# Attention and a routed expert layer on one core: w1 loaded in halves, five matmuls ahead of the first transposes, q's halves loaded ahead of k's, and v loaded three units ahead

## The chip, the cores and the metric

The kernel runs on one core of a Trainium2 chip. The time is the device time of one launch in microseconds (us); the figure to be compared is the median of several launches. TensorE (PE; its weight loads are listed as PEld), VectorE (DVE), ScalarE (ACT), GpSimd (POOL) and SyncE (SP) each run their own instructions in order and wait for one another on semaphores. Data comes from and goes to device memory by transfers (DMA) that are issued from a queue of SP, ACT or POOL and carried by 16 shared engines.

## The reference

Attention is taken within chunks of 64 rows of q, k and v (8 batches, 8 heads, 576 rows, 64 columns), and the result, seen as 4608 rows of 512, goes through a layer of 8 experts. A row takes the expert of its largest gate logit, or that of the row before it where a second, sigmoid gate says so.

```python
scores = scale * np.matmul(q_c, k_c.transpose(0, 1, 2, 4, 3))
attn = np.exp(scores - max);  attn = attn / (sum + 1e-09)
out = np.matmul(attn, v_c)
...
for b, s:                     # one after another along s
    fresh_e = argmax(x[b, s] @ w_gate)
    e = fresh_e if s == 0 or sigmoid(x[b, s] @ w_local) < 0.5 else prev_e
    h = np.maximum(x[b, s] @ w1[e], 0.0)
    out[b, s] = p[e] * (h @ w2[e])
```

## The kernel before

**Units.** The 4608 rows are worked off in 18 units of 256 rows (`NS`). For unit i the kernel loads q and k (`load_qk`, two transfers of 256 KB each) and v (`load_v`, two of 256 KB); units 6 and 15 gather their rows from four batches, and their loads are split into more and smaller transfers (eight of 128 KB for q and k, four of 128 KB for v). Then heads are paired by copies (`a_pair`, on POOL in the steady loop), q and k transposed on PE and copied out of PSUM by ACT (`a_tq`), scores multiplied and the softmax begun (`a_sa`: PE, then DVE at L244 and L247, then ACT's exponential at L252), the probabilities transposed (`a_tp`), multiplied with v and normalised into a tile `xs` (`a_va`: PE at L282, DVE at L294 to L296), and `xs` is transposed for the router (`a_tx`, `a_ra`). `a_ra` ends with a store of the unit's 256 rows of 528 floats to the scratch tensor `x_d` in device memory (L346, 528 KB, issued by SP).

**Order.** The orders are written out by hand. `PAR["start"]` fills the pipeline with units 0 to 2. `PAR["steady"]` is played for i = 1 to 15; in loop pass i PE multiplies the scores of unit i+1, the values of unit i-1, the router of unit i-2 and the transposes of unit i+2, POOL pairs unit i+3, and SP loads q and k of unit i+5 (`lq`) and v of unit i+2 (`lv`), both named at the head of the pass. `PAR["drain"]` empties the pipeline and mixes in the first tiles of the expert layer. The tokens `h0` to `h3` stand for routing work of the first half of the rows ("hooks"), which runs in passes 10 to 15. PE, DVE, ACT and POOL keep the order of these lists; SP's instructions are placed by the framework, and in the trace they stand in the order of the lists.

**Buffers.** q and k have six pairs of buffers, v has four (`vbuf`, unit i in number i mod 4), `xs` has four (`NX = 4`, unit i in number i mod 4): the values of unit j+4 write over the `xs` of unit j, so L296 of unit j+4 may write only when the store of unit j to `x_d` has left the tile. The loads from SP's and ACT's queues share eight semaphores in turn, so at most eight transfers are on their way, and the issue of a ninth waits for the first.

**Expert weights.** `load_w1(0, c)` loads one quarter of the first expert's w1 (128 x 1024 floats, 512 KB) into `raw1[c]`, behind the passes 4, 6, 8 and 10 (L880). Behind the passes 8 to 15, L885 splits one half of a quarter each (512 columns) into a rounded part (ACT, L108) and the rest (POOL, L109).

**The head of the kernel.** L588 to L593 load q and k of units 0 to 2 and v of units 0 and 1. Of unit 0, q is issued by SP and k by ACT. ACT then loads its exponential table. `ident`, the unit matrix of the transposes, is made by POOL. The first transposes (L198) wait for the first paired copies of q, made by ACT and DVE (`p0` = "AVPA": q's two copies by ACT and DVE, k's by POOL and ACT). `ps_tr` holds three PSUM tiles for transposes.

**After the drain** the expert layer's tiles follow (`two`, `body`, `rest`) with float32r products of a high and a low part (`mm1`, `mm2`, `up_pair`); only `mm1_upper` (L737) and `mm2_upper` (L755) multiply plain float32.

```python
(nc.scalar if i == 0 and src is k else nc.sync).dma_start(          # L154
```
```python
opt = dict(lq=load(qk, load_qk, i + 5) if ok(i + 5) else None,      # L871
           lv=load(vts, load_v, i + 2) if ok(i + 2) else None,
```

Of the kernel before, what the change touches and what calls it, by code (L numbers as in the profile page):

```python
# [8 lines left out]
F32 = mybir.dt.float32  # L9
# [15 lines left out]
P = 128  # L25
# [43 lines left out]
    "t0": "VAVA",  # L69
    "t1": "AAAA",  # L70
    "t2": "AVAA",
    "steady": "lq lv s*8 va*4 va s h0 tx*8 tq*8 s h1 va*4 ra*2 va h2 tq*8 ra*2 tp*8 s pr*4 h3 ",
    "hooks": [43, 43, 45, 46, 47, 48, 49, 49, 51, 51, 52, 53, 54, 55, 55, 56, 57, 58, 59, 61, 61, 62],
}

# [2 lines left out]
def tile_attention_then_moe(ctx: ExitStack, tc, q, k, v, wg, wl, w1, w2, out):  # L78
    nc = tc.nc
# [10 lines left out]
    ident = cpool.tile([P, P], F32, name="ident")  # L90
# [10 lines left out]
    def load_w1(e, c):  # L101
        nc.sync.dma_start(raw1[c], w1[e, P * c:P * c + P, :])
# [41 lines left out]
    def load_qk(i):  # L144
        qt, kt = qkbuf[i % len(qkbuf)]
        for m, (b, s0, n) in enumerate(place(i)[1]):
            for dst, src in ((qt, q), (kt, k)):
                if mixed_rows(i):
                    nc.sync.dma_start(
                        dst[m::4].rearrange("p (h n) -> p h n", h=H),  # L150
                        src[b, :, s0:s0 + n, :].rearrange("h (p r) d -> p h (r d)", r=2))
                    continue
                for j in range(2):
                    (nc.scalar if i == 0 and src is k else nc.sync).dma_start(  # L154
                        dst[:, 8 * D * j:8 * D * j + 8 * D],
                        src[b, 4 * j:4 * j + 4, s0:s0 + n, :].rearrange("g (p r) d -> p g (r d)", r=8))
        return qt, kt
# [196 lines left out]
    def ok(i):  # L354
        return 0 <= i < NS
# [144 lines left out]
    def a_pair(i, engs=(nc.gpsimd,) * 4):  # L500
        hd[i], fns = pair_heads(i, qk.pop(i), engs)
        return fns
# [19 lines left out]
    def a_tx(i, fine=False):  # L522
        xTs[i] = pa2.tile([P, 4, 256], F32, name="xT", bufs=1)
        return x_transposes(xss[i], xTs[i], fine)

    def a_ra(i, fine=False):
        return router(i, xTs.pop(i), xss.pop(i), fine)
# [66 lines left out]
    with tc.manual_schedule(engines=MAN | {ET.Pool}):  # L594
        warm = pa2.tile([P, 1], F32, name="warm", tag="xT", bufs=1)
        nc.scalar.activation(warm, ident[:, 0:1], AF.Exp)

        def load(store, fn, i):
            def go():
                store[i] = fn(i)  # L600
            return lambda: [go]

        tqs = {}

        def tq(i, g):
            if i not in tqs:
                tqs[i] = a_tq(i, ENG(PAR[f"t{i}"]))
            return tqs[i][5 * g:5 * g + 5]

        st = {f"p{i}": lambda i=i: a_pair(i, ENG(PAR[f"p{i}"])) for i in range(4)}  # L610
        st |= dict(
            s0=lambda: a_sa(0, True), q3=load(qk, load_qk, 3),
            s1=lambda: a_sa(1, True), o0=lambda: a_tp(0, True), q4=load(qk, load_qk, 4), q5=load(qk, load_qk, 5),
            v2=load(vts, load_v, 2))
        for i in range(3):
            for g in range(4):
                st[f"t{i}{'abcd'[g]}"] = lambda i=i, g=g: tq(i, g)
        st |= dict(wg=lambda: [lambda: (
            nc.sync.dma_start(wg9[:, :, 0:8], wg.rearrange("(c p) e -> p c e", p=P)),
            nc.sync.dma_start(wg9[:, :, 8:9], wl.rearrange("(c p) e -> p c e", p=P)))])  # L620
        play(PAR["start"], st)
# [242 lines left out]
    hooks = {}  # L864
    for fn, at in zip(hq, PAR["hooks"]):
        hooks.setdefault(divmod(at, 4), []).append(fn)
    man = tc.manual_schedule(engines=MAN | {ET.Pool})
    man.__enter__()
    for i in range(1, NS - 2):
        qs4 = dict(s=lambda: a_sa(i + 1), tp=lambda: a_tp(i), va=lambda: a_va(i - 1, True), tq=lambda: a_tq(i + 2))  # L870
        opt = dict(lq=load(qk, load_qk, i + 5) if ok(i + 5) else None,  # L871
                   lv=load(vts, load_v, i + 2) if ok(i + 2) else None,
                   pr=(lambda: a_pair(i + 3)) if ok(i + 3) else None, tx=(lambda: a_tx(i - 2)) if i >= 2 else None, ra=(lambda: a_ra(i - 2, True)) if i >= 2 else None)
        for h in range(4):
            opt[f"h{h}"] = (lambda h=h: [lambda: run(hooks[i, h])]) if (i, h) in hooks else None
        toks = [t for t in PAR["steady"].split() if opt.get(t.split("*")[0], 1) is not None]
        play(" ".join(toks), qs4 | {k: v for k, v in opt.items() if v is not None})
        if i == 2:
            pcol, pcol1, iota_m, iota_h, iota_hp, iota_t, iota_e, idxm8, padidx, upper, ones, zrow, notfirst, hot0 = constants()
        if i in (4, 6, 8, 10):  # L880
            load_w1(0, i // 2 - 2)
        if 8 <= i < 16:
            c, col = divmod(i - 8, 2)
            col = slice(512 * col, 512 * col + 512)
            split(w1h[c][:, col], w1l[c][:, col], raw1[c][:, col], nc.gpsimd)  # L885
# [368 lines left out]
```

## Time and profile before

| what | us |
|---|---|
| median of 3 launches | 640.31 |
| lowest, highest | 638.03, 640.63 |
| the profiled launch | 638.56 |
| its span, first to last instruction | 636.8 |
| PE busy | 608.1 (96% of the span) |
| DVE, ACT, POOL busy | 380.3, 255.8, 147.0 |

The page divides the span into 40 slices: PE is at 9 tenths or more in nearly all of them. The 16 DMA engines are at 9 tenths and above in the first ten slices (to about 160 us, the attention part) and far below in the rest. An engine's idle time is put down to what ended it ("<-"); "issue" means that it waited for nothing that the profile shows. Matmuls are pipelined, so a busy PE need not be PE at its peak.

### The profile page before, as it was taken

The page shows a single profiled execution, that of the slowest core. Times are in us where ns is not written, and L with a number is a line of the kernel's source. Part 1 is how long each engine was busy: PE and PEld are TensorE (multiplying, and loading weights), DVE is VectorE, ACT ScalarE, POOL GpSimd, SP SyncE. Part 2 cuts the span into 40 slices and gives each one's busy share as a digit, 9 for nine tenths or more (in the row PEclk, how much of TensorE's full clock was granted, in tenths as well). Part 3 has the DMA queues.
Part 4 walks back from the last instruction along what each step waited for, and adds up shares of the span by engine and source line. Part 5 has one row for each costly group of instructions (what it writes and reads, how often), then busy time and mean ns, then how long its engine had stood idle before and what let it go on. Part 6 is the DMA issues. An engine that isn't in the chain of part 4 may idle for free. (4 is left out here: it accounts for less than half of the span.)

```text
span 636.8 us, 17170 instructions
## 1 busy us (share of the span) xinstructions
PE 608.1 (96%) x5904; PEld 513.6 (81%) x5904; DVE 380.3 (60%) x990; ACT 255.8 (40%) x468; POOL 147.0 (23%) x219
## 2 busy tenths in 40 slices
PE   4899989889999999999999999999999999999995
PEld 4788777777779788789998996789888998788884
DVE  2677678887795667575434556763478533387231
ACT  4677667664421252532112443421465211343120
POOL 3353244550050302021021021031021221010201
PEclk9999999999999999999999999999999999999999
DMA  8999999998440245155021264452086511054111
GB/s 267 264 265 301 284 272 264 303 286 271 158 150 21 71 151 185 44 178 180 20 70 55 61 206 134 151 178 64 27 271 203 190 52 59 30 184 147 65 30 36
DMA packets 78355, 97.83 MB, mean 154 GB/s; under 512 B 42672, under 2 KB 46768, under 8 KB 78192
## 3 DMA queue, kind: packets, MB, share of 16 engines
q1 hardware_dynamic: 71744, 75.30, 37.9%
q0 software_dynamic: 6160, 19.99, 9.6%
q8 instruction: 84, 1.38, 0.9%
q14 instruction: 79, 0.65, 0.3%
q10 hardware_dynamic: 288, 0.52, 0.3%
HBM read 76.62 MB, written 19.69 MB: 151 GB/s over the span
## 5 line engine op out<-in xcount | busy, mean ns | idle before, releaser
L804 POOL DMA_INDIRECT out<-ysb,sidx x38 | 40.2, 1058 | 356.3 <-DVEq L1028 160.6
L743 PE MATMUL y<-w2h,hq 128*128 128x512 f32 x368 | 119.8, 395 | 1.3 <-DVE ysb L1078 1.0
L743 PEld LDWEIGHTS y<-w2h,hq 128*128 128x128 f32 x368 | 69.1, 188 | 16.9 <-issue 2.5
L743 PE MATMUL y<-w2l,hq 128*128 128x512 f32 x184 | 71.9, 391 | 0.0
L1050 PE MATMUL tr<-xp,w1h 128*128 128x256 f32 x528 | 67.0, 283 | 0.0
L1050 PEld LDWEIGHTS tr<-xp,w1h 128*128 128x128 f32 x528 | 65.5, 192 | 1.2 <-ACT w2h L1011 0.4
L743 PE MATMUL y<-w2h,hp 128*128 128x512 f32 x192 | 63.3, 397 | 0.3 <-ACT hp L690 0.3
L722 PE MATMUL h<-w1h,xp 128*128 128x512 f32 x208 | 60.5, 396 | 0.0
L1058 ACT ACTIVATE hq<-tr 128x256 fp32r<-128x256 f32 x51 | 18.9, 383 | 68.4 <-PE tr L1050 44.8
L1078 DVE TENSOR_SCALAR ysb<-y,ppr 128x512 f32<-128x512 f32 x33 | 24.8, 751 | 34.4 <-PE y L743 30.3
L722 PEld LDWEIGHTS h<-w1h,xp 128*128 128x128 f32 x208 | 38.1, 188 | 7.4
L694 POOL DMA_INDIRECT xg<-x_d,gidx x36 | 38.5, 1069 | 19.8 <-issue 14.5
L743 PEld LDWEIGHTS y<-w2h,hp 128*128 128x128 f32 x192 | 36.0, 188 | 8.1 <-ACT hp L690 0.5
L789 ACT ACTIVATE hsb<-h 128x512 f32<-128x512 f32 x26 | 14.1, 596 | 66.1 <-PE h L722 49.1
L1059 DVE SCALAR_TENSOR_TENSOR hq<-tr,hq 128x256 fp32r<-128x256 f32 x51 | 21.1, 423 | 32.3 <-ACT hq L1058 28.6
L743 PEld LDWEIGHTS y<-w2l,hq 128*128 128x128 f32 x184 | 34.6, 188 | 6.9 <-DVEq L1028 0.3
L743 PE MATMUL y<-w2l,hp 128*128 128x512 f32 x96 | 37.5, 390 | 0.0
L1018 DVE TENSOR_TENSOR w1l<-raw,w1h 128x1024 fp32r<-128x1024 f32 x28 | 32.4, 1221 | 8.3 <-ACT w1h L1011 4.9
L691 DVE TENSOR_TENSOR xp<-tr,xp 128x512 fp32r<-128x512 f32 x39 | 25.5, 686 | 18.6 <-ACT xp L690 15.8
L1050 PE MATMUL tr<-xp,w1l 128*128 128x256 f32 x264 | 35.3, 283 | 0.0
L1018 DVE TENSOR_TENSOR w2l<-raw,w2h 128x1024 fp32r<-128x1024 f32 x28 | 32.8, 1223 | 1.2 <-issue 1.2
L1050 PEld LDWEIGHTS tr<-xp,w1l 128*128 128x128 f32 x264 | 33.3, 192 | 0.0
(242 smaller groups left out, 1152.7 us busy)
## 6 DMA issues: line engine op xcount, KB each, us to landing
raw<-in_moe_w SPq DMA_DIRECT2D x72, 512.0 KB
x_d<-xs SPq DMA_DIRECT2D x16, 528.0 KB
v<-in_v SPq DMA_DIRECT2D x20, 256.0 KB
qt<-in_q SPq DMA_DIRECT2D x16, 256.0 KB
lenth<-in_q SPq DMA_DIRECT2D x16, 256.0 KB
lentl<-in_k SPq DMA_DIRECT2D x16, 256.0 KB
kt<-in_k SPq DMA_DIRECT2D x14, 256.0 KB
raw<-in_v SPq DMA_DIRECT2D x6, 256.0 KB
```

The source lines that it names most:

```text
L691: lambda: V.tensor_tensor(lo, box["ps"], hi.bitcast(F32), ALU.subtract)]
L694: nc.gpsimd.indirect_dma_start(out=dst, out_offset=None, in_=src, in_offset=bass.IndirectOffsetOnAxis(ap=gidx[t].bitcast(U32), axis=0))
L722: nc.tensor.matmul(hs[:, j], xs[a][:, c], W1[w][c][:, 512 * j:512 * j + 512], start=(c == 0 and n == 0), stop=(c == 3 and n == 2))
L743: nc.tensor.matmul(y, h_of(t, f // 4)[a][:, f % 4], W2[w][c][:, f % 2, :], start=(f == 0 and n == 0), stop=(f == 7 and n == 2))
L789: nc.scalar.activation(hsb[:, 512 * j:512 * j + 512], hs[:, j], AF.Relu)
L804: nc.gpsimd.indirect_dma_start(out=out, out_offset=bass.IndirectOffsetOnAxis(ap=sidx[t].bitcast(U32), axis=0), in_=ysb, in_offset=None, bo ...
L1018: V.tensor_tensor(lo[c], raw[c], hi[c].bitcast(F32), ALU.subtract)
L1050: nc.tensor.matmul(hb[:, 256 * n:256 * n + 256], W1[w][c][:, P * (f + n):P * (f + n) + P], XP[:, x, c].rearrange("p s t -> p (s t)"), star ...
L1058: nc.scalar.activation(hi, ps, AF.Relu)
L1059: V.scalar_tensor_tensor(lo, ps, 0.0, hi.bitcast(F32), ALU.max, ALU.subtract)
L1078: V.tensor_scalar(ysb, y, pr, None, ALU.mult)
```

## The change

w1 of the first expert comes in eight halves of a quarter (256 KB each), one in each of passes 5 to 12, right behind q and k of the pass (`lw`). Ahead of everything else PE runs five matmuls of `ident` with a broadcast `ident` (512 columns, plain float32) into a transpose tile that nobody reads. Of unit 0's q and k, SP issues the first half of each and ACT the second half of each, in the order q, k. `lv` loads v of unit i+3 instead of i+2 and stands behind the last matmuls of the values of unit i-1, which free its buffer; pass 1 loads units 3 and 4.

```diff
-    "steady": "lq lv s*8 va*4 va s h0 tx*8 tq*8 s h1 va*4 ra*2 va h2 tq*8 ra*2 tp*8 s pr*4 h3 ",
+    "steady": "lq lw s*8 va*4 va s h0 tx*8 tq*8 s h1 va*4 ra*2 va lv h2 tq*8 ra*2 tp*8 s pr*4 h3 ",
...
-                    (nc.scalar if i == 0 and src is k else nc.sync).dma_start(
+                    (nc.scalar if i == 0 and j == 1 else nc.sync).dma_start(
...
         nc.scalar.activation(warm, ident[:, 0:1], AF.Exp)
+        awake = ps_tr.tile([P, 4, P], F32, name="tr")
+        for n in range(5):
+            nc.tensor.matmul(awake, ident, ident.unsqueeze(1).to_broadcast([P, 4, P]), start=True, stop=True)
...
+    def load_piece(n):
+        c, col = n // 2, slice(512 * (n % 2), 512 * (n % 2) + 512)
+        return lambda: [lambda: nc.sync.dma_start(raw1[c][:, col], w1[0, P * c:P * c + P, col])]
...
-                   lv=load(vts, load_v, i + 2) if ok(i + 2) else None,
+                   lv=(lambda: [lambda: [load(vts, load_v, n)()[0]() for n in ((3, 4) if i == 1 else (i + 3,))]]) if ok(i + 3) else None,
...
+        opt["lw"] = load_piece(i - 5) if 5 <= i < 13 else None
...
-        if i in (4, 6, 8, 10):
-            load_w1(0, i // 2 - 2)
```

## Rows read from the trace of the kernel before

**Rows 1.** The page: engines' busy time and share; the 16 DMA engines in 40 slices.

```profile
PE 608.1 (96%) x5904; PEld 513.6 (81%) x5904; DVE 380.3 (60%) x990; ACT 255.8 (40%) x468; POOL 147.0 (23%) x219
DMA  8999999998440245155021264452086511054111
```

**Rows 2.** Windows: length; PE, PEld, DVE, ACT, POOL busy (instructions); clock, DMA share, GB/s.

```profile
40.00:60.00 20.00, 19.89 (x503) 17.04 (x504) 14.91 (x38) 15.52 (x27) 6.62 (x13) 1.00 0.99 288
...
120.00:140.00 20.00, 17.35 (x424) 14.22 (x413) 17.48 (x66) 13.57 (x24) 14.65 (x19) 1.00 1.00 269
160.00:180.00 20.00, 20.00 (x139) 15.30 (x132) 17.24 (x74) 6.29 (x13) 3.85 (x6) 1.00 0.34 112
```

**Rows 3.** Timeline of the head: start, busy us, engine, line, instruction, [idle before <-releaser].

```profile
1.43 0.28 POOL masks.py:199 TENSOR_SCALAR_AFFINE_SELECT ident<-ident 128x128 f32<-128x128 f32 x1
5.59 0.61 POOL L190 COPY kr<-kt 128x512 f32<-128x512 f32 x1 [3.87 <-DMA kt<-in_k]
6.18 0.62 ACT L188 COPY qr<-qt 128x512 f32<-128x512 f32 x1 [2.62 <-DMA qt<-in_q]
6.95 1.94 PE L198 MATMUL tr<-ident,qr 128*128 128x128 f32 x8 [6.95 <-ACT qr L188]
10.63 0.63 ACT L188 COPY kT<-tr 128x512 f32<-128x512 f32 x1 [1.07 <-PE tr L198]
11.37 1.16 PE L233 MATMUL sc<-kT,qT 64*64 64x64 f32 x64
12.95 1.09 PE L198 MATMUL tr<-ident,kr 128*128 128x128 f32 x8
18.96 1.17 POOL L190 COPY qr<-lenth 128x512 f32<-128x512 f32 x2 [2.78 <-DMA lenth<-in_q]
```

**Rows 4.** Timeline of PE: one call of `mm1_upper`, plain float32 products of 512 columns.

```profile
257.12 3.65 PE L737 MATMUL m<-raw,fullx 128*64 128x512 f32 x16
```

**Rows 5.** Timeline of SP's queue around pass 9.

```profile
90.61 1.41 SPq L102 DMA_DIRECT2D raw<-in_moe_w  x1
94.73 2.15 SPq L165 DMA_DIRECT2D raw<-in_v  x2
96.97 2.13 SPq L346 DMA_DIRECT2D x_d<-xs  x1
```

**Rows 6.** Timeline of DVE: the first write of `xs` in pass 13.

```profile
113.03 0.69 DVE L296 TENSOR_TENSOR xs<-o,rs 128x512 f32<-128x512 f32 x1
```

**Rows 7.** Windows from the start: to q's first copies, to four writes of `xs`.

```profile
0.00:6.18 6.18, 0.00 (x0) 0.00 (x0) 0.00 (x0) 1.49 (x2) 1.72 (x18) 1.00 0.63 221
...
0.00:104.57 104.57, 90.25 (x2143) 76.62 (x2144) 68.04 (x166) 69.83 (x121) 42.88 (x111) 1.00 0.95 276
0.00:113.03 113.03, 97.61 (x2317) 82.71 (x2318) 74.95 (x189) 75.65 (x131) 46.16 (x115) 1.00 0.94 275
0.00:121.69 121.69, 105.08 (x2488) 88.60 (x2489) 83.18 (x216) 81.60 (x141) 49.77 (x120) 1.00 0.94 277
0.00:130.15 130.15, 112.70 (x2663) 94.94 (x2664) 91.47 (x244) 87.71 (x152) 58.13 (x133) 1.00 0.95 277
```

**Rows 8.** Window inside pass 14, columns as in rows 2.

```profile
120.00:124.00 4.00, 4.00 (x136) 3.47 (x128) 3.79 (x17) 3.84 (x7) 2.21 (x3) 1.00 0.86 253
```

**Rows 9.** Timeline of PE: three standstills in the middle of a group of matmuls.

```profile
64.89 0.58 PE L233 MATMUL sc<-kT,qT 64*64 64x64 f32 x24 [1.44 <-issue]
80.81 0.50 PE L282 MATMUL o<-v,pT 64*64 64x65 f32 x18 [1.30 <-issue]
88.02 0.63 PE L233 MATMUL sc<-kT,qT 64*64 64x64 f32 x28 [0.64 <-issue]
```

**Rows 10.** Windows between these standstills, columns as in rows 2.

```profile
64.80:80.70 15.90, 14.62 (x378) 12.40 (x379) 10.69 (x26) 10.94 (x19) 4.94 (x9) 1.00 0.94 289
80.70:87.90 7.20, 6.57 (x126) 5.39 (x126) 5.37 (x13) 4.81 (x9) 3.36 (x5) 1.00 0.93 283
```

**Rows 11.** The page: the queues that bring code (packets, MB, share).

```profile
q8 instruction: 84, 1.38, 0.9%
```

## What the change was predicted to do

> **What bounds the kernel now.** I read the page first: PE is busy 96% of the span, the DMA engines near their limit for the first quarter and idle half the time after it [rows 1]. The windows then split the launch into two stretches. Up to about 140 us (attention) the transfers run at 0.99 to 1.00 of the engines' time and 270 to 290 GB/s, while PE is at 19.9 of 20 us between 40 and 60 and only at 17.35 between 120 and 140; from 160 on PE has 20.00 of 20 and the transfers 0.34 [rows 2]. So the expert layer runs at PE's pace, no operation of it changes, and all that the change does shows as an earlier or later end of the attention part: a microsecond there is a microsecond of the total, if it reaches the end of the loop.
>
> Two things can hold the loop. One is the chain of PE, DVE and ACT: in pass 14 PE is busy 4.00, ACT 3.84 and DVE 3.79 of 4 us, so a delay of DVE there isn't made up [rows 8]. The other is the stream of transfers. A time can be read off it by counting bytes, with q and k of a unit at 1.05 MB, v at 0.52, a store at 0.54 and a quarter of w1 at 0.52. Up to and including the store of unit 7, SP has queued 15 units of q and k, 12 of v, 8 stores and three quarters of w1: 27.9 MB (the order is that of pass 9: w1, q, k, v, store [rows 5]). When unit 11 first writes over that `xs`, at 104.57, the engines have moved 104.57 us x 276 GB/s = 28.9 MB, of it some 0.5 of code (a third of what the code queue brings in all [rows 11]). The store is ahead by 0.46 MB. The same account for the writes at 113.03 [rows 6], 121.69 and 130.15 (rates 275, 277, 277; queued 30.05, 32.7 and 34.8 MB) leaves 0.55, 0.50 and 0.69 MB [rows 7]. A moved byte isn't yet a landed transfer: q and k of unit 0 are 1.05 MB, and when their last half is used at 6.18 the engines had moved 221 x 6.18 = 1.37 [rows 3, 7], a lag of 0.3 MB. So the stores land 0.2 to 0.4 MB, some 0.6 to 1.4 us, before they are needed. Nothing waits for them, but PE couldn't run much faster either: whatever it gains ahead of pass 12 beyond about 0.6 us would end in a wait for a store.
>
> **The head.** The matmuls on `ident` can start when POOL has made it, at 1.71 us, with a semaphore's time about 1.8 [rows 3]. Their price: one call of `mm1_upper` is 8 plain float32 products of 512 columns, two always side by side on 64 columns of the array; it shows 16 records, two a product, and takes 3.65 us [rows 4]. So one step is 3.65/4 = 0.91 us at the full clock and 1.82 at half. That the array starts at half clock shows in its durations, though the page's clock column says 1.00 there: 8 transposes take 1.94 us at 6.95 and 1.09 at 12.95, and the first scores at 11.37 take 1.16 [rows 3]. Five products take 4.6 us all at the full level and 9.1 all at half; they end between 6.4 and 10.9. As the clock rose in the trace of before while the first transposes ran, I take half of the work at each level: about 6.8 us, an end at 8.6. From the first transposes to the scores it is now 4.4 us (6.95 to 11.37); at the full clock 16 transposes need 2.2 and the last copy 0.63 [rows 3], so 2.8. The first scores then start at 8.6 + 2.8 = 11.4, where they start now. **I enter 0**, with ends of -2.2 and +2.3.
>
> The 2.8 us stand on transposes that keep the full level. If they let it fall back, the 4.4 us of now stay, the scores start at 13.0, and the head costs 1.6. Against that, PE ran nothing but transposes ahead of 11.37, and the scores there, 64 records in 1.16 us, have the pace of later ones, 24 in 0.58 and 28 in 0.63 [rows 3, 9]. The Trainium skill's page "TensorE: Matmul & The Clock Gate", Part 4, has a rule for the first reading: transposes don't count as activity, and the full clock doesn't engage for them. By that rule the head is +1.6 (an estimate from these rows); the trace disagrees with it.
>
> q ahead of k: q's copies start at 6.18 now, k's first at 5.59 [rows 3]. With both halves of q as the first two transfers, q's copies could start when k's now do or before; PE is then still in the five products, so this is covered by them. Without them it would be worth 0.6 us or somewhat more. k comes about 0.6 later and is needed only after q's transposes. Four transfers stay four, two of them on ACT, ahead of its table load as now. What is next in line also caps a gain here: at 18.96 POOL has waited 2.78 us for q of unit 3 [rows 3], a transfer that starts no earlier.
>
> **w1 in pieces.** Four issues of 512 KB become eight of 256 on SP, the same bytes. SP pays four more issues of at most 1.4 us each [rows 5], and spends most of such a time waiting for one of the eight transfers on their way; while the engines are at 0.99 it isn't SP that is short. Each piece now stands ahead of v and the store of its pass instead of behind the store of every second one. Its reader is ACT's split three passes later. Counted in bytes, piece 6 (pass 11) is the 31.9th MB, and ACT needs it in pass 14, near 121.69, when 33.2 MB net of code have moved [rows 7]: covered by 1.3 MB, less the lag of 0.3, or some 3 us. If that cover were gone, ACT would wait, and DVE and PE behind it. I enter 0.
>
> **v three units ahead.** The new wait is SP's, for the values of unit i-1 in pass i; behind it on SP stand the store of unit i-2 and the next q and k. It is over when SP gets there: the values of unit 8 run on PE at 80.81 [rows 9], and SP reaches v of the same pass at 94.73 [rows 5]. That wait costs 0; were SP level with PE, it would stand through the first part of each pass, some 4 of the 7 us between two of them [rows 9], with the store behind it. The price is the order: 0.52 MB of v that stood behind a store now stand ahead of it, in every pass from 1 to 14. With w1, whose pieces are either level with before or one piece behind, the stores of units 7, 8, 9 and 10 have 0.26, 0.52, 0.26 and 0.52 MB more ahead of them. Of the leads above (0.46, 0.55, 0.50, 0.69, each less the lag of 0.3) this leaves -0.10, -0.27, -0.06 and -0.13 MB. The largest counts once, since a wait in pass 13 moves the later writes too: 0.27 MB at 277 GB/s is **1.0 us**. DVE waits at L296 in pass 13, behind it are its softmax steps, and PE and ACT follow. The ends are 0 (the lag is smaller) and 1.9 (the whole 0.52 MB). q and k are needed a pass after POOL pairs them, so 0.5 MB doesn't reach PE there. What v gains, no one waits for: no wait on v is in the trace.
>
> **Code.** PE's standstills of 1.44, 1.30 and 0.64 us lie inside groups of equal matmuls, with no releaser [rows 9]. Between them it ran 378 + 379 and 126 + 126 matmuls and weight loads [rows 10]; with the few semaphore instructions that aren't counted these are 768 and 256, and the code queue brings 1.38 MB in 84 packets, 16.4 KB each [rows 11], 64 bytes for each of 256. So PE stood because the next block of code had not come past the full queues. The five products add 20 instructions and shift every boundary; by 130 us PE has passed 20 of them [rows 7], and where the next standstills fall is drawn anew. I enter 0, with ends of -3.4 (these three gone) and +3.5 (as many again). The Trainium skill's page "Runtime: NRT & Kernel Launch", Instruction fetch mechanics, calls the cost of crossing such a boundary mostly hidden; by that this term is 0 with no ends, and the rivals B and C below have no chance. The trace disagrees by the 3.4 us of rows 9.
>
> **Sum.** 638.56 for the profiled launch (span 636.8 and 1.8 around it) + 0 + 0 + 1.0 + 0 = 639.6. The median lies 1.75 above the profiled launch, so 641.3.
>
> **The rivals.** (A) The stores stay in time and PE's start pays: the five products run mostly at the full clock. For it speaks that the lag is known from the head alone; against it that it needs both terms at once. The gain ends at the lead of the stores, some 0.8 us: 639.5. (B) Slower: the new code boundaries fall into the bursts of scores and values. It decides once three or four more of some 20 boundaries catch PE with less than a block's transfer in hand, at about 1 us each: 641.3 + 3 = 644.3. (C) Faster: smaller transfers of w1 let code past sooner, and the standstills of rows 9 vanish. Against it: the bytes per pass are the same, and a PE that is early would wait for the stores. It needs the stores to come earlier too: 640.3 - 3.5 = 636.8. (D) The change doesn't do what it says: SP's order is not written by hand, and v may be placed where it stood; then 640.3. (E) The clock falls back under the transposes: 641.3 + 1.6 = 642.9, the reading that the rows above speak against.
>
> **How the numbers follow.** A measurement of this kernel can tell about 0.5%, 3.2 us, from no change. Forecast 0.47, A 0.17, B 0.15, C 0.12, D 0.05, E 0.04. Forecast, A, D and E are within 0.5%: 0.73; slower 0.15 (B), faster 0.12 (C). The range takes in the ends of the three open terms as far as they don't pile up, and about half of B and C: 636.8 to 644.0.
>
> **What would show it.** Right: DVE's L296 in pass 12 or 13 waits for a transfer of `x_d`; the first scores within 1 us of 11.4, with PE's first transposes after 8; the span of the part after 160 us unchanged. Wrong: first scores before 9.5 with the lead kept to 135 us; no wait for a store (the account by bytes is off); passes 7 to 10 without standstills at whole multiples of 256 instructions; or a wait of ACT for w1.

## The result and the profile after

| | before | after |
|---|---|---|
| median of 12 launches of each | 638.82 | 644.24 |
| lowest, highest | 637.53, 641.01 | 641.77, 648.18 |
| the profiled launch | 638.56 | 642.65 |
| its span | 636.8 | 640.9 |

The changed kernel takes 1.0080 times the time of the one before (95% interval 1.0061 to 1.0099): about 5 us slower. The forecast was 641.3. It started from a median of three launches (640.31) that was 1.5 us above that of twelve, and added 1.0; measured are 5.4 between the medians and 4.1 between the profiled launches. Of all launches of the study one, of the kernel called "the last one with the new head" below, took 699.58 us at a granted clock of 0.81 and is left out of the ratios.

The page and the windows after, which answer [rows 1, 2], have the same shape as before: the attention part is full of transfers, and from 160 us on PE is at 19.9 of 20.

```profile
PE 614.6 (96%) x5914; PEld 514.9 (80%) x5914; DVE 379.0 (59%) x990; ACT 256.3 (40%) x468; POOL 146.9 (23%) x219
DMA  8899898998531155056021164451177511054201
```

```profile
40.00:60.00 20.00, 20.00 (x503) 17.10 (x505) 15.11 (x38) 15.73 (x27) 6.58 (x13) 1.00 0.95 282
120.00:140.00 20.00, 16.95 (x375) 14.15 (x375) 18.32 (x63) 12.71 (x23) 13.06 (x19) 1.00 1.03 283
160.00:180.00 20.00, 19.87 (x114) 15.21 (x113) 16.57 (x68) 7.19 (x14) 2.62 (x5) 1.00 0.48 151
```

**Where the 4.1 us came from.** The first product of `mm1` starts at 146.98 before and at 150.10 after, 3.1 us later. From it to the start of the last product of `mm2` pass 483.5 and 483.6 us. The remaining 0.9 is the end from there on, 6.3 us before and 7.2 after; in other kernels of this study, whose work there is the same, it was 6.0 to 7.8. So 3.1 us of the attention part have to be explained.

**The head** (timeline of PE and of ACT's first copy, for [rows 3]): q's copies start at 4.68 in place of 6.18, the five products end at 8.9, the scores start 0.2 us later than before.

```profile
1.77 7.15 PE L599 MATMUL tr<-ident 128*128 128x512 f32 x10 [1.77 <-POOL ident masks.py:199]
4.68 0.62 ACT L188 COPY qr<-qt 128x512 f32<-128x512 f32 x1 [1.11 <-DMA qt<-in_q]
8.76 1.04 PE L198 MATMUL tr<-ident,qr 128*128 128x128 f32 x8
11.57 1.16 PE L233 MATMUL sc<-kT,qT 64*64 64x64 f32 x64 [0.27 <-ACT kT L188]
```

**DVE now waits for stores.** The timeline of DVE shows L296 waiting for the transfer of `x_d` in seven consecutive passes, 8 to 14, for 6.5 us in all. In the trace before no L296 has such a bracket (for [rows 6], at 113.03, it shows none).

```profile
73.11 0.69 DVE L296 TENSOR_TENSOR xs<-o,rs 128x512 f32<-128x512 f32 x1 [1.03 <-DMA x_d<-xs]
81.70 0.69 DVE L296 TENSOR_TENSOR xs<-o,rs 128x512 f32<-128x512 f32 x1 [1.78 <-DMA x_d<-xs]
89.28 0.69 DVE L296 TENSOR_TENSOR xs<-o,rs 128x512 f32<-128x512 f32 x1 [0.77 <-DMA x_d<-xs]
97.95 0.69 DVE L296 TENSOR_TENSOR xs<-o,rs 128x512 f32<-128x512 f32 x1 [1.84 <-DMA x_d<-xs]
106.27 0.69 DVE L296 TENSOR_TENSOR xs<-o,rs 128x512 f32<-128x512 f32 x1 [0.61 <-DMA x_d<-xs]
116.54 0.69 DVE L296 TENSOR_TENSOR xs<-o,rs 128x512 f32<-128x512 f32 x1 [0.28 <-DMA x_d<-xs]
125.98 0.69 DVE L296 TENSOR_TENSOR xs<-o,rs 128x512 f32<-128x512 f32 x1 [0.20 <-DMA x_d<-xs]
```

**What PE waited for.** The view of waits groups PE's idle time by what ended it (us in total, times, longest). From 10 us to the first product of `mm1`, before, its first rows:

```profile
PE sc L233 <- issue: 3.4, 5, 1.4
PE o L282 <- issue: 2.0, 2, 1.3
PE lg L333 <- DVE lT L329: 1.4, 2, 0.8
...
PE o L282 <- DVE xs L296: 0.6, 2, 0.3
```

and after:

```profile
PE lg L333 <- DVE lT L329: 3.6, 6, 1.1
PE o L282 <- DVE xs L296: 2.6, 5, 1.0
PE o L282 <- issue: 1.4, 3, 0.8
...
PE tr L436 <- DVE cinT L431: 1.3, 1, 1.3
```

All rows added up: waits without a releaser ("issue", the standstills of [rows 9]) fall from 6.1 to 1.8 us, waits for DVE rise from 3.4 to 9.4, the sum from 12.3 to 14.1. The three standstills of [rows 9] are gone, and more than their time came back behind DVE.

**And the clock fell once.** PE's timeline in pass 12 after:

```profile
106.60 1.12 PE L198 MATMUL tr<-ident,qr 128*128 128x128 f32 x8 [0.38 <-ACT xT L188]
109.02 0.18 PE L436 MATMUL tr<-ident,cinT 1*18 1x1 f32 x2 [1.30 <-DVE cinT L431]
109.13 0.95 PE L282 MATMUL o<-raw,pT 64*64 64x65 f32 x32
110.01 1.08 PE L324 MATMUL lg<-xT,wg 128*32 128x256 f32 x8
111.02 1.96 PE L198 MATMUL tr<-ident,kr 128*128 128x128 f32 x8
```

the same groups before:

```profile
107.31 0.18 PE L436 MATMUL tr<-ident,cinT 1*18 1x1 f32 x2 [0.72 <-ACT qT L188]
107.42 0.69 PE L282 MATMUL o<-raw,pT 64*64 64x65 f32 x32
108.05 0.64 PE L324 MATMUL lg<-xT,wg 128*32 128x256 f32 x8
108.62 1.09 PE L198 MATMUL tr<-ident,kr 128*128 128x128 f32 x8
```

and windows of 1 us after (the third column from the end is the granted clock, 0.50 being 1.2 of 2.4 GHz):

```profile
109.00:110.00 1.00, 0.98 (x34) 0.86 (x34) 1.00 (x3) 0.00 (x0) 0.00 (x0) 0.71 0.66 195
110.00:111.00 1.00, 1.00 (x12) 0.20 (x8) 0.60 (x4) 0.00 (x0) 0.00 (x1) 0.50 0.84 168
111.00:112.00 1.00, 1.00 (x9) 0.98 (x6) 0.78 (x4) 0.00 (x0) 1.00 (x2) 0.50 0.82 219
112.00:113.00 1.00, 1.00 (x7) 1.00 (x6) 0.61 (x1) 0.62 (x1) 0.16 (x1) 0.58 1.10 271
```

Behind two waits, 0.38 and 1.30 us, PE ran three groups at the lower level: from L282 to L333 it took 3.65 us (109.13 to 112.78) in place of 2.13, 1.5 us more. The waits (+1.8) and the clock (+1.5) add up to 3.3, against the 3.1 us to be explained.

The wait for `cinT` comes from the store. From the start of L296 to the copy that makes `cinT` DVE takes 2.44 us before (104.57 to 107.01) and 2.45 after (106.27 to 108.72); L296 starts 0.61 us late after, and PE's wait grows by 0.58, from 0.72 to 1.30. The other traces say the same: in all seven kernels where L296 waits in pass 12, for 0.33 to 1.26 us, PE's wait for `cinT` is 0.67 to 0.69 us longer than L296's.

**The stores.** SP's queue around the store of unit 7 after, for [rows 5]: its issue begins at 99.06 in place of 96.97 and ends 3.8 us later, at 102.91. v, now ahead of it, takes 1.00 us for its two issues.

```profile
97.29 0.58 SPq L872 DMA_DIRECT2D raw<-in_moe_w  x1
97.97 1.00 SPq L165 DMA_DIRECT2D v<-in_v  x2
99.06 3.85 SPq L346 DMA_DIRECT2D x_d<-xs  x1
```

It isn't this store alone. The timelines of SP and DVE give, for the stores that passes 8 to 11 wait for, when the issue ends and when L296 wants to write over the tile (its start less its wait for `x_d`); the head alone is a kernel of the next section.

| store of unit | issue ends: before | after | head alone | L296 wants it: before | after | head alone |
|---|---|---|---|---|---|---|
| 3 | 66.23 | 69.52 | 67.74 | 73.36 | 72.08 | 70.78 |
| 4 | 73.61 | 78.22 | 76.49 | 81.79 | 79.92 | 79.61 |
| 5 | 82.70 | 85.79 | 84.64 | 89.67 | 88.51 | 87.70 |
| 6 | 90.55 | 93.88 | 93.41 | 96.83 | 96.11 | 95.48 |

The lines of unit 4, SP before and after and DVE before (DVE after is the one at 81.70 above):

```profile
71.20 2.41 SPq L346 DMA_DIRECT2D x_d<-xs  x1
75.45 2.77 SPq L346 DMA_DIRECT2D x_d<-xs  x1
81.79 0.69 DVE L296 TENSOR_TENSOR xs<-o,rs 128x512 f32<-128x512 f32 x1
```

After, these stores come 3.1 to 4.6 us later, and L296 asks for them 0.7 to 1.9 us earlier. The delay is there before any L296 waits: the issue for unit 0 ends at 45.61 in place of 42.11.

### The profile page after: what moved, and what is told of

Read it like the earlier page. It is cut to its first block, busy times and chain, and to the rows that moved or that the text cites. A ratio compares the mean times of both kernels' runs of the same rounds, so it can differ in the third digit from the quotient of the medians.

```text
span 640.9 us, 17210 instructions
## 1 busy us (share of the span) xinstructions
PE 614.6 (96%) x5914; PEld 514.9 (80%) x5914; DVE 379.0 (59%) x990; ACT 256.3 (40%) x468; POOL 146.9 (23%) x219
## 5 line engine op out<-in xcount | busy, mean ns | idle before, releaser
L792 ACT ACTIVATE hsb<-h 128x512 f32<-128x512 f32 x26 | 14.1, 596 | 66.1 <-PE h L725 49.1
```

The lines of the kernel that those rows point to most:

```text
L792: nc.scalar.activation(hsb[:, 512 * j:512 * j + 512], hs[:, j], AF.Relu)
```

## The experiments

The theory at the outset was that the stores come late, because v and w1 stand ahead of them on SP; the rivals were the new order of the first loads and the code's new block boundaries. Each ratio is against launches of the kernel before on the same chip, with its 95% interval. The waits come from the one profiled launch of each kernel, the medians from 5 to 12 launches; a launch of one kernel differs from the next by up to 8 us, so a profile shows which waits a kernel has, not how much its median pays for each. Five of the profiled launches are at an end of their kernel: the quickest for w1's pieces alone, w1 late, w1 among small pieces and the stores by ACT in the kernel before, the slowest for half of w1. The last column is on record for every launch: how many have a mean granted clock of 0.995 or less.

| kernel | ratio | PE, "issue" | PE, behind DVE | L296 for `x_d` | first `mm1` product | clock 0.995 or less |
|---|---|---|---|---|---|---|
| before | 1 | 6.1 | 3.4 | 0 | 146.98 | 6 of 85 |
| after | 1.0080 (1.0061 to 1.0099) | 1.8 | 9.4 | 6.5 | 150.10 | 9 of 12 |
| v alone | 1.0038 (1.0008 to 1.0067) | 2.2 | 5.6 | 2.0 | 145.79 | 5 of 12 |
| head alone | 0.9994 (0.9969 to 1.0019) | 0.7 | 4.9 | 2.5 | 146.31 | 2 of 12 |
| w1's pieces alone | 1.0060 (1.0035 to 1.0085) | 0.9 | 5.7 | 1.6 | 145.99 | 4 of 12 |
| after, w1 in whole chunks | 1.0052 (1.0029 to 1.0076) | 4.7 | 7.5 | 3.6 | 150.62 | 9 of 12 |
| after, store ahead of v | 1.0147 (1.0113 to 1.0181) | 7.2 | 6.8 | 4.1 | 155.00 | 5 of 6 |
| before, w1 late but whole | 1.0020 (0.9999 to 1.0040) | 1.7 | 4.9 | 0.8 | 145.37 | 0 of 10 |
| before, w1 split in place | 1.0012 (0.9989 to 1.0036) | 1.6 | 7.3 | 1.6 | 147.16 | 0 of 10 |
| before, half of w1 left out | 0.9994 (0.9976 to 1.0013) | 5.4 | 4.0 | 0 | 148.04 | 0 of 11 |
| before, w1 among small pieces | 0.9979 (0.9955 to 1.0003) | 2.8 | 4.0 | 0 | 144.25 | 0 of 11 |
| the last one with the new head | 1.0030 (1.0005 to 1.0054) | 4.0 | 4.1 | 0.4 | 147.62 | 8 of 11 |
| after, stores by ACT | 1.0189 (1.0164 to 1.0214) | 1.2 | 5.6 | 0 | 158.73 | 5 of 5 |
| before, stores by ACT | 1.0072 (1.0047 to 1.0098) | 2.8 | 5.8 | 0 | 149.76 | 2 of 6 |

In the traces a fall of the clock inside the work takes 1.7 us of full clock away, 0.0027 of the mean; one behind the last product, where PE has nothing left to do, costs nothing and takes up to 2.1 us, 0.003. So a mean of 0.995 or less has a fall inside the work. Such launches are 6 of 85 of the kernel before (on the three chips of the experiments) and 9 of 12 of the changed kernel, and every kernel that is slower by more than its interval has some. They are the longer ones: in the median 645.4 against 642.1 in the changed kernel, 643.1 against 639.5 with v alone, 643.8 against 640.6 with w1's pieces alone. So the clock goes with the loss in many launches. It isn't all of it: the six launches of w1's pieces alone at 0.998 or more take 640.1 in the median, against 638.0 before. And what stood ahead of a fall is seen only where there is a trace.

**One part at a time.** v alone, on the kernel before:

```diff
-    "steady": "lq lv s*8 va*4 va s h0 tx*8 tq*8 s h1 va*4 ra*2 va h2 tq*8 ra*2 tp*8 s pr*4 h3 ",
+    "steady": "lq s*8 va*4 va s h0 tx*8 tq*8 s h1 va*4 ra*2 va lv h2 tq*8 ra*2 tp*8 s pr*4 h3 ",
...
-                   lv=load(vts, load_v, i + 2) if ok(i + 2) else None,
+                   lv=(lambda: [lambda: [load(vts, load_v, n)()[0]() for n in ((3, 4) if i == 1 else (i + 3,))]]) if ok(i + 3) else None,
```

> The kernel before with one edit: v loaded three units ahead, issued behind the values that free its buffer. Theory (late stores): in the changed kernel every store to x_d stands behind one more unit of v on SP's queue, which at the 0.52 MB of a v unit and the 262 to 295 GB/s of the changed kernel's slices from 80 to 140 us is 1.8 to 2.0 us, and DVE's L296 then waits for the store four units back (six waits of 0.20 to 1.84 us from 81.70 to 125.98 and one of 1.03 at 73.11, 6.5 us in all). If v is the cause, this kernel alone is 3 to 6 us slower than before and its L296 waits for x_d in at least four passes. Rival (head): the v edit alone costs under 1.5 us and L296 waits in at most two passes. Rival (code blocks): slower with no wait of L296 for x_d but with PE standstills marked issue that before doesn't have.

Measured 640.45, 1.0038 or 2.4 us: less than the theory's 3 to 6 and more than the rival's 1.5. L296 waits in three passes, one fewer than the theory and one more than the rival had it, for 2.0 us, the longest 1.26, and the clock falls behind the wait for `cinT`, 1.93 us, here too (0.84 and 0.74).

```profile
103.43 0.69 DVE L296 TENSOR_TENSOR xs<-o,rs 128x512 f32<-128x512 f32 x1 [1.26 <-DMA x_d<-xs]
```

```profile
104.00:108.00 4.00, 2.07 (x45) 0.97 (x42) 3.68 (x14) 0.96 (x2) 0.00 (x0) 0.84 0.69 177
108.00:112.00 4.00, 4.00 (x67) 3.74 (x67) 2.11 (x7) 2.44 (x5) 2.33 (x4) 0.74 1.13 312
```

The head alone:

```diff
-                    (nc.scalar if i == 0 and src is k else nc.sync).dma_start(
+                    (nc.scalar if i == 0 and j == 1 else nc.sync).dma_start(
+        awake = ps_tr.tile([P, 4, P], F32, name="tr")
+        for n in range(5):
+            nc.tensor.matmul(awake, ident, ident.unsqueeze(1).to_broadcast([P, 4, P]), start=True, stop=True)
```

> The kernel before with one edit: five plain products on PE in front, and q ahead of k as the first loads. Theory (late stores): the head hands on its 0.2 us (first scores 11.57 for 11.37) and the five products shift code blocks; within 1.5 us of before, no wait of L296 for x_d. Rival (head): the new order of the first loads delays unit 6's pieces (27.20 to 34.5 on SP in the changed kernel, 26.83 to 32.9 before), the DMA share from 24 to 36 us falls (0.77, 0.70, 0.61 for 0.90, 0.85, 0.87), all later stores land some 1.7 us late, and this kernel alone is 2 us or more slower.

Measured 637.32, 0.9994. The rival's price for the order of the first loads, 2 us or more, falls. But the theory's "no wait of L296" was wrong, and this is the most telling trace of the study. v and w1 stand where they stood before, PE has hardly a standstill (0.7 us), and L296 waits for a store in seven passes all the same, 2.5 us; PE also waits 2.0 us for v. Two of the seven:

```profile
62.97 0.69 DVE L296 TENSOR_TENSOR xs<-o,rs 128x512 f32<-128x512 f32 x1 [0.32 <-DMA x_d<-xs]
96.12 0.69 DVE L296 TENSOR_TENSOR xs<-o,rs 128x512 f32<-128x512 f32 x1 [0.64 <-DMA x_d<-xs]
```

Two things meet there (the table of stores above). The stores' issues end 1.5 to 2.9 us later than in the trace before, much as the rival had it, and L296 wants the tiles 1.4 to 2.6 us earlier, with the standstills gone. Whether the head makes the stores late is open: with w1 late, split, in pieces or half left out the queue of SP up to the store of unit 0 is that of the kernel before, and its issue ends at 42.66 to 44.76 there, at 42.11 in the trace before and at 44.99 here. A delay of this size comes from launch to launch too, and the trace before has the earliest of these.

w1's pieces alone:

```diff
+        opt["lw"] = load_piece(i - 5) if 5 <= i < 13 else None
-        if i in (4, 6, 8, 10):
-            load_w1(0, i // 2 - 2)
```

> The kernel before with one edit: w1's four chunks as eight pieces, one in each of passes 5 to 12. Theory (late stores): 0.26 MB less is ahead of the stores of units 3 to 6, so these land up to 1 us earlier; nothing waits for them before, so the time is within 1.5 us of before, and no wait of L296 for x_d. Rival (w1): the last pieces come later than the chunks did, the splits on GpSimd wait for them and the drain starts late, 2 us or more slower.

Measured 641.97, 1.0060, 3.8 us slower: the largest of the three parts, and the one that both forecast and theory had put at nothing. Its splits on GpSimd aren't late (PE stands 0.4 us behind one of them, and the first `mm1` product of the profiled launch starts at 145.99), so the rival's reason is not seen either. The profiled launch was the quickest of its twelve (638.94), so its five waits of L296 (1.6 us) and PE's 1.5 us for v are what a quick launch has. What the others lose, apart from the clock of four of them, isn't in a trace. The three parts add up to 2.4 + 3.8 - 0.4 = 5.8 us, against 5.1 by the ratio of the whole.

**The store ahead of v**, in the changed kernel:

```diff
-    "steady": "lq lw s*8 va*4 va s h0 tx*8 tq*8 s h1 va*4 ra*2 va lv h2 tq*8 ra*2 tp*8 s pr*4 h3 ",
+    "steady": "lq lw s*8 va*4 va s h0 tx*8 tq*8 s h1 va*4 ra*2 va h2 tq*8 ra*2 lv tp*8 s pr*4 h3 ",
```

> The changed kernel with one edit: the issue of v for three units ahead stands behind the store to x_d in each pass, in place of ahead of it. Theory (late stores): SP no longer holds the store behind the wait for v's buffer nor behind 0.52 MB of v, the stores land 2 to 4 us earlier, the seven waits of L296 for x_d (6.5 us) fall to under 1.5 us in all, and the kernel is 3 us or more faster than the changed one: within 1.5 us of before or faster. Rival (head, or code blocks): the stores' place isn't the cause, the time stays within 2 us of the changed kernel, some 643 to 645.

Measured 648.29, 1.0147: 4 us slower than the changed kernel, against the theory. The timeline of SP shows where the time of the issues went:

```profile
76.48 0.38 SPq L346 DMA_DIRECT2D x_d<-xs  x1
76.96 2.05 SPq L165 DMA_DIRECT2D v<-in_v  x2
79.06 5.59 SPq L154 DMA_DIRECT2D qt<-in_q  x2
```

The store's own issue shrinks to 0.38 us, v and then q behind it take 2.05 and 5.59, and the 40 us from 80 on move 253 GB/s in place of 278. Waits of L296 fall from 6.5 to 4.1, and 7.2 us of standstills come, one of 2.09 us at 65.48 with the clock at 0.72 in the 4 us around it. By what SP was held there the trace doesn't settle, and so not why the kernel is slower.

**Bytes or order?** After these four I thought that the stream of transfers as a whole bounds the attention part.

```diff
-        if i in (4, 6, 8, 10):
+        if i in (4, 6):
             load_w1(0, i // 2 - 2)
+        if i == 3:
+            for c in (2, 3):
+                nc.gpsimd.memset(raw1[c], 0.0)
+        if i in (8, 10):
+            nc.sync.dma_start(raw1[i // 2 - 2][:, 0:64], w1[0, P * (i // 2 - 2):P * (i // 2 - 1), 0:64])
```

> The kernel before with half of w1's first load left out: the third and fourth chunk bring 64 of their 1024 columns, the rest is set to zero by GpSimd, so the first expert's products are not the reference's; 0.98 MB less is moved ahead of the first product of mm1_upper's loop (L722 in the kernel before). Theory (the stream of loads bounds the front): in five of the six kernels read so far the first such product starts when 40.5 to 41.2 MB have been moved (146.98 us at 280 GB/s before, 150.10 at 274 in the changed one, 145.79 at 278 with v alone, 146.31 at 277 with the head alone, 145.99 at 280 with w1's pieces alone; 155.00 at 259 with the store first is 40.1), so 0.98 MB less at 280 GB/s is 3.5 us less: some 634.5 beside 638. Rival (waits in the engines' order bound the front): nothing waits for w1's chunks there, so within 1 us of before.

Measured 638.35, 0.9994 (0.9976 to 1.0013): 0.98 MB less moved, nothing gained, and the theory falls in this form. The trace, of the slowest of its eleven launches, has no wait of L296; it has standstills, 5.4 us, one of them longer than any before. The edit also puts two fills of 1.84 us together on GpSimd at 42.88, and what these cost was not measured apart.

```profile
68.61 0.58 PE L233 MATMUL sc<-kT,qT 64*64 64x64 f32 x24 [2.54 <-issue]
```

w1's chunks among the eight small pieces of units 6 and 15:

```diff
+                    if src is k and m in (0, 2):
+                        load_w1(0, 2 * (i // 9) + m // 2)
```

> The kernel before with w1's four chunks moved to stand among the small pieces of the mixed units: chunks 0 and 1 among the eight pieces of unit 6, chunks 2 and 3 among those of unit 15. Theory (the stream bounds the front): while SP issues eight pieces of 128 KB at 0.60 to 0.66 us each it brings 200 GB/s to a stream that takes 280 to 300, and the share falls to 0.77 at 30 to 34 us and to 0.45 to 0.74 at 102 to 108 us; a chunk of 512 KB takes one issue of 0.46 us, so two chunks in each place fill up to 2.5 us of it: 1 to 4 us faster than before. Rival (late stores): chunks 0 and 1 stand ahead of the stores of units 0 to 3, which now land 3.7 us later, L296 waits for x_d, 1 to 3 us slower.

Measured 637.09, 0.9979 (0.9955 to 1.0003): 1.3 us, at the edge of what can be told from nothing. The hole is filled as expected (before the window 102 to 108 has a share of 0.62 and 165 GB/s):

```profile
102.00:108.00 6.00, 4.90 (x141) 3.83 (x134) 4.61 (x17) 3.47 (x6) 1.26 (x1) 1.00 0.94 263
```

and L296 waits for no store, which goes against the rival. With the head of the changed kernel on top:

> The kernel before with two edits that each came out at or under before: w1's chunks among the pieces of the mixed units (alone 0.9979, 0.9955 to 1.0003) and the changed kernel's head (alone 0.9994). If they add: 1 to 3 us faster than before, some 636.5. Rival: the front's end is set by chains that neither touches; within 1 us of before.

Measured 641.69, 1.0030 (1.0005 to 1.0054). Two edits that each came out at or just under before are together slower than it. Effects of this size don't add here; no version of the study is shown to beat the kernel before. The profiled launch, at a clock of 0.998, is not one of the eight at 0.995 or less, which take 641.7 in the median; the other three are at 638.3 to 640.6.

**Why w1's pieces cost.** Whole chunks at the pieces' place, and halves at the chunks' place:

```diff
+        opt["lw"] = (lambda: [lambda: load_w1(0, (i - 5) // 2)]) if i in (5, 7, 9, 11) else None
-        if i in (4, 6, 8, 10):
-            load_w1(0, i // 2 - 2)
```

> The kernel before with w1's chunks whole, but at the place of the pieces: at the head of passes 5, 7, 9 and 11 behind q and k, in place of behind the store in passes 4, 6, 8 and 10. With e3_w1_only (pieces at the head of passes 5 to 12: 4.0 us slower) it tells lateness from the count of loads. Theory (later loads leave the stream empty early and full late): 2 to 4 us slower than before. Rival (four loads more for SP and twice the semaphores): within 1 us of before.

```diff
         if i in (4, 6, 8, 10):
-            load_w1(0, i // 2 - 2)
+            for col in (slice(0, 512), slice(512, 1024)):
+                nc.sync.dma_start(raw1[i // 2 - 2][:, col], w1[0, P * (i // 2 - 2):P * (i // 2 - 1), col])
```

> The kernel before with each of w1's chunks as two loads of half the columns, one directly behind the other, at the chunk's own place. Theory (later loads): the place is unchanged, within 1 us of before. Rival (count): SP takes two issues of 0.6 us for one of 0.46 and a packet of 2 KB for one of 4 KB, four times; 2 to 4 us slower, as e3_w1_only.

Measured 639.43 (1.0020) and 639.39 (1.0012): 1.3 us for the place and 0.8 for the count, neither clear of zero, and together less than the 3.8 of both, though within the intervals. The place was to cost 2 to 4 us by its theory, the count 2 to 4 by its rival: neither is borne out by itself; how the cost of the pieces divides stays open.

The changed kernel with w1's whole chunks put back:

```diff
-        opt["lw"] = load_piece(i - 5) if 5 <= i < 13 else None
+        if i in (4, 6, 8, 10):
+            load_w1(0, i // 2 - 2)
```

> The changed kernel with w1 put back: four whole chunks behind the stores of passes 4, 6, 8 and 10; v three ahead and the new head stay. If the parts add (v alone +2.2 us mean, head alone -0.3, w1 alone +3.9): some 2 us above before and 3 to 4 below the changed kernel, 640 to 641. Rival (v and w1 only hurt together, or v alone carries the whole): 643 or more. The chunks in passes 4, 6 and 8 put 0.26 to 0.52 MB more ahead of the stores than the pieces do, so by late stores alone L296's waits would not shrink from the 6.5 us of the changed kernel.

Measured 642.86, 1.0052 or 3.3 us, between the two expectations. The interval holds the sum of v and head (2.0 us) and leaves 1.8 us, uncertain by as much, for the pieces inside the whole. L296 still waits 3.6 us in its trace, where the theory of late stores had it stay at 6.5.

**The stores on ACT's queue**, in the next pass behind ACT's copies of qT, in the changed kernel and in the one before:

```diff
-    "steady": "lq lw s*8 va*4 va s h0 tx*8 tq*8 s h1 va*4 ra*2 va lv h2 tq*8 ra*2 tp*8 s pr*4 h3 ",
+    "steady": "lq lw s*8 va*4 va s h0 tx*8 tq*8 st s h1 va*4 ra*2 va lv h2 tq*8 ra*2 tp*8 s pr*4 h3 ",
...
-                nc.sync.dma_start(xv[b, s0:s0 + n].rearrange("(c p) n -> p c n", p=P), xs)
+                if hold[0]:
+                    held.append(lambda: nc.scalar.dma_start(xv[b, s0:s0 + n].rearrange("(c p) n -> p c n", p=P), xs))
...
+        opt["st"] = (lambda: [lambda: [held.pop(0)() for _ in list(held)]])
```

> The changed kernel with one edit: each steady pass's store to x_d is issued by ACT, in the next pass behind ACT's copies of qT, in place of by SP behind v. ACT waits there 1.5 to 2.2 us a pass for the transposes of k, and one issue is 0.60 to 0.65 us. Theory (late stores: with the code fetches' standstills gone, DVE's L296 waits for the store four units back, because that store stands behind SP's loads): the stores land 2 us or more earlier, the seven waits of L296 (6.5 us) shrink to under 2 us in all, and the kernel is 2 to 4 us faster than the changed one, 640 to 642. Rival (the front is slower for another reason, and L296's waits only take up slack): within 1 us of the changed kernel, 643.5 to 645, though the waits of L296 shrink.

> The same edit on the kernel before, as the control: nothing waits for the stores there, so what it costs or brings by itself shows here. Theory (late stores): within 1 us of before, since no L296 waits. Rival (ACT's issues delay its copies, or SP's loads without the stores between them run further ahead): 1 us or more to either side.

Measured 652.02 (1.0189) and 644.08 (1.0072): the first outside both expectations. L296 waits for no store any more, but the edit brought a larger wait of its own, so it tells nothing on what L296's waits were worth. The timeline of ACT in the first of the two:

```profile
66.83 1.13 ACT L188 COPY kT<-tr 128x512 f32<-128x512 f32 x2 [4.15 <-DMA lentl<-in_k]
77.99 1.14 ACT L188 COPY kT<-tr 128x512 f32<-128x512 f32 x2 [5.48 <-DMA v<-in_v]
```

The store just ahead of each copy is held until a load of SP's has landed, since the transfers of both queues share eight semaphores; ACT's copies stand behind it, and PE waits 11.8 us for them. The control's larger cost is as the rival expected.

**Not tried:** a fifth buffer for `xs`, laid into the tiles of w2 that are empty until 137 us. It would take away L296's wait without changing any queue's order, and would say directly how much of the loss is that wait.

## Why the prediction was right or wrong

**Bounds.** Right: the part from the first product of `mm1` to the last of `mm2` is the same to 0.1 us, and 3.1 of the 4.1 us are in the attention part. Right too, and used too little, was the sentence that PE couldn't run much faster there, because a gain ahead of pass 12 would end in a wait for a store. The head alone shows much of that: 6.1 us of standstills shrink to 0.7 and the time stays, since PE waits 2.0 us for v, 1.5 more behind DVE and 0.8 more behind ACT.

**The head, 0.** Right. The products end at 8.9 for 8.6, the scores start at 11.57 for 11.4, and alone the head is 0.9994. That the transposes keep the full level behind the products, against Part 4 of the Trainium skill's page "TensorE: Matmul & The Clock Gate", the trace after bears out: eight of them take 1.04 us at 8.76. Rival E falls with it. The clock did fall, but in pass 12, where no step of the prediction looked.

**w1's pieces, 0.** Wrong by the most. The cover of 3 us was worked out for the one reader of w1, ACT's split, and it held: ACT waits for no piece in the trace after. For the stores the pieces were counted too, in the term of v, as level or a help. What the step left out is what they do to the other loads behind them on SP's queue: alone, PE waits 1.5 us for v in the profiled launch, and before for none. Alone they cost 3.8 us (2.2 to 5.4). By which wait is not settled; the clock shows a fall in four of twelve launches.

**v three ahead, +1.0.** Right in kind; alone it measured 2.4 us (0.5 to 4.3), an interval that holds the 1.0. SP's new wait for the values costs nothing, as said, and the late store holds L296, as said. The four writes for which I had counted the bytes, those of passes 12 to 15, wait 0.61, 0.28, 0.20 and 0 us, 1.1 in all. That this is near 1.0 is partly luck: passes 8 to 11 had waited 1.03, 1.78, 0.77 and 1.84 us before them, 5.4 in all, and I had made no account for these.

The failed step is the delay of the stores. By bytes it was 0.26 or 0.52 MB in turn, 0.9 or 1.9 us; counted in the same way it is the same for the stores that passes 8 to 11 wait for, and these come 3.1 to 4.6 us later. Some 1.4 to 2.7 us of that are not v's or w1's bytes. The head, entered as 0, has a delay of 1.5 to 2.9 us in its own trace, and launches with the same queue differ by up to 2.7, so the cause of this part stays open. A smaller part is on the other side. In passes 7, 9 and 10 of the trace before PE stands still 1.44, 1.30 and 0.64 us [rows 9], and a pass that stands still gives its store that much more time; with them gone, L296 asked 0.7 to 1.9 us earlier. The leads were read in one trace, with its standstills and its early stores; the standstills were entered as a term by themselves, and the early stores not at all.

**Code blocks, 0 between -3.4 and +3.5.** The standstills fell by 4.3 us, more than the whole 3.5 of rival C, and the time went up. Rival C had said itself that such a gain needs the stores to come earlier too; they came later. In the profiles of this study a kernel with few standstills mostly waits for stores (head alone, w1 split), and one that doesn't wait for stores has standstills (before, half of w1); only w1 among the small pieces has little of both (2.8 and 0), in the quickest of its launches. The Trainium skill's page "Runtime: NRT & Kernel Launch", Instruction fetch mechanics, calls such a crossing mostly hidden; the stops of 2.54 and 2.09 us in two of the runs disagree, as [rows 9] did. They stand where the 1.44 of [rows 9] stood: the 2.54 with the same 24 matmuls of the group left, the 2.09 with 33 left, in a kernel whose five products put some 20 instructions ahead.

**The clock, not entered.** 1.5 us in the profiled launch. The waits for stores reach PE in pass 12 through DVE's routing chain (`cinT`, 1.30 us), and behind that wait PE runs three groups at half clock. The slower clock cost more (1.5) than the wait ahead of it had grown (from 0.72 to 1.30). By its mean clock, nine of this kernel's twelve launches have such a fall.

**The rivals.** A, C and D are out: the time rose, and SP's order is the one written. B, the slower one, named 644.3, and 644.24 was measured, but for another reason: standstills were fewer, not more. What was said to show the forecast right came (L296 waits in passes 12 and 13, scores within 1 us of 11.4, the part after 160 us unchanged), and so did one sign against it (passes 7 to 10 with no standstill over 0.44 us). Both belong to the same account. The range ended at 644.0 because terms were not let pile up; v, the pieces and the clock did, and the median, 644.24, is just outside.

**What is open.** That L296's waits are the loss, and not only stand where standstills stood, is argued from the traces and not shown: the edits that moved the stores brought waits of their own. Why the stores come later than the bytes say is open too. Shown is that v and the pieces each cost time by themselves and the head doesn't, that L296's wait in pass 12 reaches PE in nearly its full length, that the slower kernels have more launches with a fallen clock, and that taking 0.98 MB out of the stream brings nothing.

## What to carry to other kernels

Where several limits lie within a microsecond of one another, the slack read in a trace holds only at the pace of that trace: take the standstills out first, then ask what is late, in every pass and not only where a wait is already near. It holds for that launch, too: read the same times in a second one before a lead of half a microsecond is relied on. Loads put ahead on one in-order queue with a fixed number of transfers on their way delay all that stands behind them there; cost each edit by its effect on the stores, not on its own reader. And try the parts of such a change one at a time: here the one thought to be free cost the most.

## What the runs showed of the hardware

- The same five plain float32 products took 6.26 to 7.59 us in the six kernels that have them, with the same start (1.77 or 1.78; 7.15 in the changed kernel, 6.26 with the head alone): how much of them ran at the lower level (by the prediction's estimate 4.6 us are all at the full and 9.1 all at the lower) differs from one to the next, and the first scores follow, from 10.68 to 12.02.
- Behind a wait of 1.30 us the clock was at 0.50 to 0.71 for 4 us; behind a standstill of 1.44 us in the trace before it stayed at 1.00 (64 to 68 us). The length of one wait doesn't decide. Of the fourteen traces' waits for `cinT` in pass 12 the eight of 0.70 to 1.04 us brought no fall, those of 1.30, 1.46, 1.72 and 1.93 did, and two of 1.47 did not. In the kernel with the stores on ACT a wait of 4.04 us at 78.66 brought 0.50, and one of 2.71 at 67.49 did not (64 to 72 us at 1.00); a standstill of 2.09 us at 65.48 brought 0.50 (store ahead of v), one of 2.54 at 68.61 did not (half of w1).
- An issue on ACT can be held 5.48 us by a load that another queue has issued, when the two share a semaphore; a queue that is free is not yet a transfer that starts.
